# Block-sparse attention and a two-matrix expert layer on one Trainium2 core: four weight blocks ahead instead of five, copies of v and of whole rows laid out anew, two splits issued sooner

## The chip, the cores and the metric

The kernel runs on one core of a Trainium2 chip. The time is that of the device for one execution, in microseconds (us). A core has a matrix engine (PE, with its weight loads shown as PEld), a vector engine (DVE), a scalar engine (ACT), a general engine (POOL), a queue engine for transfers (SP) and 16 DMA engines. Each engine takes its own instructions in the order in which they were written; semaphores tie the engines to each other. Operands of PE, DVE, ACT and POOL lie in an on-chip memory (SBUF) of 128 partitions, and PE writes its sums into another one (PSUM), here eight banks of 128 x 512 fp32.

## What is computed

```python
scores = scale * q @ k.T            # 4 batches, 8 heads, 768 tokens, head size 64
mask   = |block_i - block_j| <= 1  or first/last block row or column  or sampled block
attn   = softmax(where(mask, scores, -1e9))     # blocks of 32 tokens, 24 block rows,
x      = (attn @ v) as 3072 x 512               # three sampled blocks per block row
out    = (max(x @ w_in, 0) ** 2) @ w_out        # w_in 512 x 2048, w_out 2048 x 512
```

The sampled blocks are data. The weights come in double precision and are cut to fp32 on the chip.

## The kernel before

The 3072 tokens are 24 tiles of 128 (six to a batch), and three tiles make a chunk; there are eight chunks c = 0..7. Two kinds of work run in one stream on PE.

**The expert layer** of a chunk (`moe`) goes through 16 column blocks f. `hidden(c, f)` is 12 matmuls `ph` of 128x384 (L888): each fp32 operand is split into a high and a low part, and three of the four products are kept. `finish` then makes r (ACT, L909), gh (ACT, L915), gf (DVE, L920) and gl (POOL, L922). `project(c, f)` is 9 matmuls `po` of 128x512 (L941), gh with the high and the low part of w_out's block, gl with the high part; it runs LEAD = 2 blocks behind `hidden`. So at a chunk turn, `project` of blocks 14 and 15 of chunk c-1 stand back to back between `hidden(c-1, 15)` and `hidden(c, 0)`, and nothing but attention can be put between them. Chunk 0 uses plain fp32 for `project` (`po` at L931, on gp from L912), which needs no split of w_out and no gl.

The weights are split by `split` into a tile `wi` or `wo` of two halves: the high part by a CAST (L850 on ACT in chunk 0, L852 on DVE later), the low part by a subtraction on POOL (L853). A split is made anew in every chunk. Where each is issued sets what it stands behind on DVE and POOL. `wi` of block 1 of a chunk is split after the turn has begun (in `moe(c)`, ahead of `project(c-1, 14)`), `wo` of block f just ahead of `hidden(c, f)`.

In the prologue and in chunk 0 the weights are also cut. `cut_next` runs a little pipeline over 32 raw blocks `craw` of 512 KB: the load (L790, on POOL's queue) at step `done`, two ACT operations (`cut`, L806 and L808) AHEAD steps later, two bit operations on DVE (`cut_bits`, L817 and L818) one step after that. Raw blocks, splits `wi` and `wo`, and the rows `pg`, `pgm` of whole blocks share WBUFS = 7 buffers of one tag, `w`, which go round in the order of request.

**Attention.** The rows of a tile are done in two halves (`Half`; q block rows 1..22 with their eight key blocks), the rows of a batch's first and last block, which see all keys, in four `Whole` units. A half goes through scores `s` (PE, L436), row maxima `m` and `p` = s - m (DVE, L448 and L457) or the exponent on ACT (L498), exponents and block copies `pm` (ACT, L482), a transpose (DVE, L488; in the prologue and for the halves of tiles 3 to 5 on PE with copies `pT`, L523 on ACT and L525 on DVE), values `pv` (PE, L534) and a norm (DVE, L548 to L551). A whole unit goes through `g` (PE, L629), maxima (DVE, L643 to L647), exponents `pg` (ACT), `move` (16 copies `pgm` of 32x192, L665, eight on POOL and eight on ACT), a transpose `pTg` (DVE, L671), `pvg` (PE, L699) and a norm (L710 to L718).

**What sets the order.** The program is written in its final order by hand: `moe(c)` is a generator that yields some 96 times a chunk, and at each yield the `Stream` of attention takes one step. A unit starts at the step that `units` gives it: a half every 16 steps, beginning EARLY = 23 steps ahead of the chunk before; whole unit i of an even chunk G_AT steps after half i. LAG says how many steps lie between a unit's parts ("t" from `g` of a whole unit to its `move`, "w0" and "w" to its transpose and its values). Attention of chunk c thus runs under the expert layer of chunk c-1. Attention of chunk 0 is a prologue, with units every five steps; in it the V tiles are filled by POOL, by ACT (`fixed`, L212) and by sampled DMAs on SP (L365), whose offsets are read from a table.

PSUM's tag "s" of five banks is shared by `ph`, `s`, `g`, `pv` and `pvg`, in turn; three banks hold `po`.

Of the kernel before, what the change touches and what calls it, by code (L numbers as in the profile page):

```python
# [52 lines left out]
AHEAD = 5  # L53
# [12 lines left out]
LAG = {"s": 0, "e": 4, "v": 11, "x": 4, "t": 4, "c": 0, "v0": 13, "w0": 4, "w": 19, "n": -1}  # L66

G_AT = 6
# [7 lines left out]
CUT_0 = range(30, 61, 5)  # L76
CUT_1 = 3
# [4 lines left out]
FIXED_0 = 14  # L82
# [14 lines left out]
def tile_block_sparse_attention_moe(ctx: ExitStack, tc, kd, knd, qd, qgd, vd, vnd, samp, const, wcat, out):  # L97
# [282 lines left out]
    class Half:  # L380
# [63 lines left out]
        def maxima(self):  # L444
# [7 lines left out]
            if not self.moved:  # L452
                if self.k >= UC:
                    nc.vector.tensor_scalar(m[at], m[at], -SCALE, None, op0=ALU.mult)
                return
# [36 lines left out]
        def exps(self):  # L492
            at = self.rows
            if self.k < UC:
                nc.scalar.mul(self.m[at], self.m[at], -SCALE)
            for e in range(2):
                for i in range(2):
                    nc.scalar.activation(  # L498
                        self.p[at, 2 * e + i].rearrange("p c a s -> p (c a s)"),
                        self.sb[e][at, i * NSLOT : (i + 1) * NSLOT],  # L500
                        AF.Exp,
                        scale=SCALE,
                        bias=self.m[at, e, i : i + 1],
                    )
# [81 lines left out]
    class Whole:  # L586
# [71 lines left out]
        def move(self):  # L658
# [3 lines left out]
            for g in range(NJ):  # L662
                for a in range(NJ):
                    copy = nc.scalar.copy if a % 2 else nc.gpsimd.tensor_copy
                    copy(self.pm[a * BLK : (a + 1) * BLK, g], x[g * BLK : (g + 1) * BLK, :, a])  # L665
                    if a % 2:
                        yield 0
# [59 lines left out]
    def units(c):  # L727
# [9 lines left out]
        both += [(at + i * STEP + G_AT, u) for i, u in enumerate(wholes)]  # L737
# [226 lines left out]
    def moe(c):  # L964


        if 0 < c < NCH:
            for i in range(UC):
                high(c, i, 0, NCC, nc.scalar.copy)
                low(c, i, 0, NCC)  # L970
        if c > 0:
            yield 0.7
            if c < NCH:
                wi1[c, 1] = split(c, W1[1], f"wi{c}_1")
# [7 lines left out]
        for f in range(NF):  # L982
            for n in (f, f + 1) if f == 0 else (f + 1,):
                if n < NF:
                    if c == 0:
                        need(n, 0)
                    if n in SINGLE and (c, n) not in wi1:
                        wi1[c, n] = split(c, W1[n], f"wi{c}_{n}")
            if c == 0 and f == 0:
# [6 lines left out]
            if c > 0:  # L996
# [35 lines left out]
    def prepare():  # L1032
# [7 lines left out]
        load_sampled(2, 1, nc.sync, SP, (0, 1))  # L1040
        key_windows(2, 1, nc.gpsimd.tensor_copy)
        deque(keys[2], 0)
        for f in windows(2, 1):
            f(nc.gpsimd.tensor_copy)
# [8 lines left out]
    while work.todo or work.running:  # L1053
        work.step(now)
        now += 1
        if now >= FIXED_0 and fixed:
# [19 lines left out]
    for c in range(NCH + 1):  # L1076
        work.drain(c, now)
        for _ in moe(c):
# [3 lines left out]
            if c == 0 and now % CUT_1 == 0 and done < len(cuts) + AHEAD + 2:  # L1082
# [64 lines left out]
```

## Time and profile before

| | us |
|---|---|
| three timed runs | 742.28, 743.63, 744.39 (median 743.63) |
| the profiled execution's own time | 742.05 |
| its span, first to last instruction | 740.2 |
| PE busy | 706.8 (95%) |
| PEld, weight loads beside PE | 566.4 (77%) |
| POOL busy | 550.6 (74%) |
| DVE busy | 528.7 (71%) |
| ACT busy | 503.9 (68%) |

The mean granted clock of PE is 0.998 of full speed. The prologue, attention of chunk 0, lasts to about 53 us of the span; chunk 0 of the expert layer to about 156; the turns into chunks 2 to 7 lie at about 245, 328, 417, 500, 589 and 672; after 640 there is no attention left. In a list of instructions, the figure in brackets is how long the engine stood idle before the row, with what ended it. PE's matmuls are pipelined, so that one row's duration overlaps the next one's start.

### The profile page before, as it was taken

What the parts mean: (1) busy time and instruction counts of PE and PEld (TensorE: products, weight loads), DVE (VectorE), ACT (ScalarE), POOL (GpSimd) and SP (SyncE); (2) the same over time, 40 slices, a digit from 0 to 9 for tenths busy, and PEclk for the clock granted to TensorE, in tenths of its full rate; (3) what the DMA queues carried; (4) which work ended last, traced back from release to release, by engine and by line L of the source; (5) the groups of instructions that cost most, each with busy time, mean ns of one, the idle gap of its engine ahead of it and who ended that gap; (6) DMA issues with size and microseconds to landing.
All of it is one profiled execution on the core that took longest, in us unless ns stands there. A gap on an engine that the chain in (4) does not pass through costs nothing.

```text
span 740.2 us, 21520 instructions
## 1 busy us (share of the span) xinstructions
PE 706.8 (95%) x7496; PEld 566.4 (77%) x7496; DVE 528.7 (71%) x1062; ACT 503.9 (68%) x1116; POOL 550.6 (74%) x710
## 2 busy tenths in 40 slices
PE   5769999999999999999999999999999999999997
PEld 2546665668788888877878888887778888889895
DVE  5787767868686868668776877768777686647542
ACT  6976777988865866589776776578776767532222
POOL 8978839348876677869777577777877577868984
PEclk9999999999999999999999999999999999999999
DMA  9786798555635565646445467555455352101001
GB/s 282 211 255 172 227 323 245 143 143 158 179 97 134 164 176 159 150 105 158 130 127 136 103 190 196 156 115 158 104 157 145 93 163 49 33 1 43 1 1 43
DMA packets 92784, 104.05 MB, mean 141 GB/s; under 512 B 13667, under 2 KB 80484, under 8 KB 92676
## 3 DMA queue, kind: packets, MB, share of 16 engines
q1 hardware_dynamic: 86724, 79.82, 40.9%
q0 software_dynamic: 5664, 22.45, 9.2%
q8 instruction: 60, 0.98, 0.6%
q14 instruction: 48, 0.39, 0.2%
q10 hardware_dynamic: 288, 0.39, 0.1%
HBM read 96.32 MB, written 6.29 MB: 139 GB/s over the span
## 4 chain that ended last, share of the span: by engine, by line
PE 71%; DVE 9%; ACT 8%; DMA 4%; POOL 3%; SPq 3%; issue 2%; ACTq 0%; POOLq 0%; DVEq 0%
PE ph L888 30%; PE po L941 27%; PE pv L534 5%; PE s L436 5%; DMA V<-in_v_dram 3%; PE po L931 2%; DMA q<-in_q_dram 2%; SPq L365 2%; ACT craw L808 1%; DVE m L448 1%; PE pvg L699 1%; PE g L629 1%; ACT p L498 1%; ACT r L909 1%; POOL gl L922 1%
## 5 line engine op out<-in xcount | busy, mean ns | idle before, releaser
L888 PE MATMUL ph<-xh,wi 128*128 128x384 f32 x960 | 275.1, 347 | 0.2 <-ACT p L498 0.2
L482 ACT ACTIVATE pm<-p 32x256 f32<-32x256 f32 x528 | 219.2, 415 | 15.1 <-DVE p L457 7.9
L941 PE MATMUL po<-wo,gh 128*128 128x512 f32 x672 | 211.7, 396 | 0.1
L853 POOL TENSOR_TENSOR wi<-W,wi 128x512 fp32r<-128x512 f32 x120 | 163.4, 1362 | 62.8 <-DVE wi L852 37.9
L888 PEld LDWEIGHTS ph<-xh,wi 128*128 128x128 f32 x960 | 174.1, 188 | 22.4 <-issue 12.0
L909 ACT ACTIVATE r<-ph 128x384 f32<-128x384 f32 x128 | 63.0, 492 | 167.5 <-PE ph L888 167.0
L853 POOL TENSOR_TENSOR wo<-WO,wo 128x512 fp32r<-128x512 f32 x112 | 144.7, 1292 | 34.4 <-DVE wo L852 33.1
L922 POOL TENSOR_TENSOR gl<-gf,gh 128x384 fp32r<-128x384 f32 x112 | 118.8, 1061 | 64.6 <-DVE gf L920 55.8
L888 PE MATMUL ph<-xl,wi 128*128 128x384 f32 x480 | 161.8, 337 | 0.0
L941 PEld LDWEIGHTS po<-wo,gh 128*128 128x128 f32 x672 | 123.0, 188 | 27.1 <-issue 7.5
L941 PE MATMUL po<-wo,gl 128*128 128x512 f32 x336 | 134.5, 400 | 5.0 <-POOL gl L922 4.9
L920 DVE SCALAR_TENSOR_TENSOR gf<-ph,r 128x384 f32<-128x384 f32 x112 | 62.0, 554 | 108.0 <-ACT r L909 100.0
L888 PEld LDWEIGHTS ph<-xl,wi 128*128 128x128 f32 x480 | 90.2, 188 | 8.9 <-issue 5.2
L852 DVE CAST wo<-WO 128x512 fp32r<-128x512 f32 x112 | 86.3, 771 | 0.0
L941 PEld LDWEIGHTS po<-wo,gl 128*128 128x128 f32 x336 | 63.0, 187 | 24.7 <-POOL gl L922 11.4
L915 ACT ACTIVATE gh<-r 128x384 fp32r<-128x384 f32 x112 | 58.9, 526 | 10.1
L534 PEld LDWEIGHTS pv<-V,pT 128*32 128x32 f32 x2816 | 43.2, 110 | 29.0 <-ACT pT L523 12.6
L448 DVE TENSOR_REDUCE m<-s 128x2 f32<-128x512 f32 (+1 forms) x96 | 61.0, 675 | 2.7 <-PE s L436 2.7
L534 PE MATMUL pv<-V,pT 128*32 128x65 f32 x2816 | 52.6, 223 | 9.5 <-ACT pT L523 6.5
L852 DVE CAST wi<-W 128x512 fp32r<-128x512 f32 x105 | 60.2, 574 | 0.0
L436 PE MATMUL s<-KG,q 64*32 64x256 f32 x1408 | 53.4, 382 | 1.0 <-ACT pT L523 1.0
L931 PE MATMUL po<-WO,gp 128*128 128x512 f32 x96 | 46.8, 602 | 0.0
(93 smaller groups left out, 770.3 us busy)
## 6 DMA issues: line engine op xcount, KB each, us to landing
craw<-in_w_dram POOLq DMA_DIRECT2D x32, 512.0 KB, 5.2
V<-in_v_dram SPq DMA_DIRECT2D x462, 32.5 KB, 2.3
KG<-in_k_dram SPq DMA_DIRECT2D x189, 64.0 KB, 1.9
V<-in_v_dram SPq DMA_DIRECT2D x28, 390.0 KB, 6.3
KG<-in_k_dram SPq DMA_DIRECT2D x12, 768.0 KB, 5.8
q<-in_q_dram SPq DMA_DIRECT2D x24, 256.0 KB, 2.9
out_dram<-ot SPq DMA_DIRECT2D x22, 256.0 KB, 5.2
V<-in_v_dram SPq DMA_DIRECT2D x16, 292.5 KB, 5.9
```

What stands on the lines that cost most here:

```text
L436: nc.tensor.matmul(self.sb[e][g * BLK : (g + 1) * BLK, i * NSLOT : (i + 1) * NSLOT], q[r, j, pr, :], kg[r, j, :, pr, :], start=True, stop= ...
L448: nc.vector.tensor_reduce(m[at, e], self.sb[e][at].rearrange("p (i c) -> p i c", i=2), axis=AX, op=ALU.max)
L482: nc.scalar.activation(p[a * BLK : (a + 1) * BLK, g], x[g * BLK : (g + 1) * BLK, :, a], AF.Exp, scale=SCALE)
L534: nc.tensor.matmul(po[h * BLK : (h + 1) * BLK, g * VW : (g + 1) * VW], self.pT[:, g, 2 * e + i, c], v[:, self.u, j, h * VW : (h + 1) * VW] ...
L852: nc.vector.tensor_copy(w[:, 0], src)
L853: nc.gpsimd.tensor_tensor(w[:, 1], src, w[:, 0], op=ALU.subtract)
L888: nc.tensor.matmul(ph[c, f][:, :TOK], wi[:, w, cc], x[:, cc], start=(cc == 0 and i == 0), stop=(cc == NCC - 1 and i == 2),)
L909: nc.scalar.activation(r, acc[:, :TOK], AF.Relu)
L920: nc.vector.scalar_tensor_tensor(gf, acc[:, :TOK], 0.0, r, op0=ALU.max, op1=ALU.mult)
L922: nc.gpsimd.tensor_tensor(gl, gf, gh, op=ALU.subtract)
L931: nc.tensor.matmul(acc[c][u], g[:, u * P : (u + 1) * P], WO[f], start=(f == 0), stop=(f == NF - 1))
L941: nc.tensor.matmul(acc[c][u], g[:, at], w[:, k], start=(f == 0 and i == 0), stop=(f == NF - 1 and i == 2))
```

## The change

1. AHEAD is 4, not 5. Each raw block is cut one step of the pipeline sooner after its load; `prepare` issues four loads first, not five; CUT_0 has four steps in the prologue, not seven, and CUT_1 steps every second yield for the first 12 yields of chunk 0 and every third after that.
2. FIXED_0 spreads ACT's nine copies into V and the loads after them over the steps 10 to 31 of the prologue (before: one at every step from 14 on). In `prepare` POOL's window copies of the last V tile go ahead of the last key copies.
3. The scaling of `m` by -SCALE for the halves of tiles 3 to 5, six instructions, goes from DVE (L454) to ACT (L495).
4. `move` yields after each of 12 copies, not after each of 8. LAG "t", "w0" and "w" are shortened so that "t" + `move` + "w0" + "w" stays 35. G_AT is a table: whole units start 6, 30, 50 and 68 steps after the first half rather than 6, 22, 38 and 54.
5. At a chunk turn, `wo` of block 0 is split before xh and xl of the new chunk are made, and `wi` of block 1 of the next chunk is split at f = 15 of the chunk before, ahead of `project(c, 13)`, rather than after the turn.

The instructions of PE are the same in number and kind; they stand in another order. DVE has six fewer, ACT six more.

```diff
--- before.py
+++ after.py
@@ -50,7 +50,7 @@
 TOK = UC * P
 LEAD = 2
 PRE = 4
-AHEAD = 5
+AHEAD = 4
 WBUFS = 7
 
 SINGLE = tuple(range(1, NF))
@@ -63,9 +63,9 @@
 STEP = PIECES // (2 * UC)
 EARLY = 23
 LAST = 4
-LAG = {"s": 0, "e": 4, "v": 11, "x": 4, "t": 4, "c": 0, "v0": 13, "w0": 4, "w": 19, "n": -1}
-
-G_AT = 6
+LAG = {"s": 0, "e": 4, "v": 11, "x": 4, "t": 2, "c": 0, "v0": 13, "w0": 3, "w": 18, "n": -1}
+
+G_AT = (6, 30, 50, 68)
 
 STEP_0 = 5
 STEP_1, FIRST_1 = 12, 4
@@ -73,13 +73,13 @@
 LAG_0 = {"s": 2, "x": 2, "t": 3, "c": 2, "v0": 2, "n": 2, "r": 1, "l": 3, "l0": 8}
 SPLIT_0 = 52
 
-CUT_0 = range(30, 61, 5)
-CUT_1 = 3
+CUT_0 = range(30, 46, 5)
+CUT_1 = {0: 2, 1: 3}
 
 KEYS_0 = 8
 
 
-FIXED_0 = 14
+FIXED_0 = (10, 15, 20, 21, 25, 26, 27, 28, 31)
 KEYS_3 = range(40, 56, 4)
 MOVED = 6
 
@@ -450,8 +450,6 @@
                 )
             self.p = rot.tile([P, 4, 2, NJ, BLK], F32, tag="p", name=f"p{self.name}", bufs=PBUFS)
             if not self.moved:
-                if self.k >= UC:
-                    nc.vector.tensor_scalar(m[at], m[at], -SCALE, None, op0=ALU.mult)
                 return
             for e in range(2):
                 nc.vector.tensor_tensor(
@@ -491,8 +489,7 @@
 
         def exps(self):
             at = self.rows
-            if self.k < UC:
-                nc.scalar.mul(self.m[at], self.m[at], -SCALE)
+            nc.scalar.mul(self.m[at], self.m[at], -SCALE)
             for e in range(2):
                 for i in range(2):
                     nc.scalar.activation(
@@ -663,7 +660,7 @@
                 for a in range(NJ):
                     copy = nc.scalar.copy if a % 2 else nc.gpsimd.tensor_copy
                     copy(self.pm[a * BLK : (a + 1) * BLK, g], x[g * BLK : (g + 1) * BLK, :, a])
-                    if a % 2:
+                    if a > 0:
                         yield 0
 
         def turn_blocks(self):
@@ -734,7 +731,7 @@
             return [(i * STEP_1 + FIRST_1, u) for i, u in enumerate(halves)]
         at = begins(c - 1) - EARLY
         both = [(at + i * STEP, u) for i, u in enumerate(halves)]
-        both += [(at + i * STEP + G_AT, u) for i, u in enumerate(wholes)]
+        both += [(at + G_AT[i], u) for i, u in enumerate(wholes)]
         return sorted(both, key=lambda x: x[0])
 
     class Stream:
@@ -965,13 +962,12 @@
 
 
         if 0 < c < NCH:
+            split_wo(c, 0)
             for i in range(UC):
                 high(c, i, 0, NCC, nc.scalar.copy)
                 low(c, i, 0, NCC)
         if c > 0:
             yield 0.7
-            if c < NCH:
-                wi1[c, 1] = split(c, W1[1], f"wi{c}_1")
             for f in range(NF - LEAD, NF):
                 if c == 1 and f == NF - 1:
                     split_wo(0, f)
@@ -986,6 +982,8 @@
                         need(n, 0)
                     if n in SINGLE and (c, n) not in wi1:
                         wi1[c, n] = split(c, W1[n], f"wi{c}_{n}")
+                elif c + 1 < NCH:
+                    wi1[c + 1, 1] = split(c + 1, W1[1], f"wi{c + 1}_1")
             if c == 0 and f == 0:
                 for n in range(2):
                     yield from half_hidden(c, n, 0, NCC // 2)
@@ -993,7 +991,7 @@
                 split_wo(c, f - 1)
             if f >= LEAD:
                 yield from project(c, f - LEAD)
-            if c > 0:
+            if c > 0 and f > 0:
                 split_wo(c, f)
             yield from hidden(c, f)
 
@@ -1038,10 +1036,12 @@
             f(nc.gpsimd.tensor_copy)
         load_sampled(1, 0, nc.sync, SP, (2,))
         load_sampled(2, 1, nc.sync, SP, (0, 1))
+        for _ in range(NJ):
+            next(keys[2])
+        for f in windows(2, 1):
+            f(nc.gpsimd.tensor_copy)
         key_windows(2, 1, nc.gpsimd.tensor_copy)
         deque(keys[2], 0)
-        for f in windows(2, 1):
-            f(nc.gpsimd.tensor_copy)
 
     fixed = [lambda copy, k=k, i=i: copy_static(k, i, copy) for k in range(UC) for i in range(2)]
     fixed += windows(2, 0)
@@ -1053,7 +1053,7 @@
     while work.todo or work.running:
         work.step(now)
         now += 1
-        if now >= FIXED_0 and fixed:
+        if now in FIXED_0:
             fixed.pop(0)(nc.scalar.copy)
             if not fixed:
                 load_sampled(2, 1, nc.sync, SP, (2,))
@@ -1079,7 +1079,7 @@
             now += 1
             if later and next(later[0], True):
                 later.pop(0)
-            if c == 0 and now % CUT_1 == 0 and done < len(cuts) + AHEAD + 2:
+            if c == 0 and now % CUT_1[now >= 12] == 0 and done < len(cuts) + AHEAD + 2:
                 cut_next()
             if now < begins(c + 1) - LAST:
                 work.step(now)
```

Three places show what moved. The first is on ACT in chunk 0, around the cast of the high part of `wi` of block 4 (an engine's name with a number is the semaphore that an instruction waits for; `W` and `WO` are fp32 blocks after the cut). Before:

```order
L808 ACTIVATE craw_1_1201<-craw_1_1201,below 128x512
L850 CAST wi_4_1522<-W_83 128x512 [waits DVE_49,Activation_49]
L806 ACTIVATE W_1318<-craw_0_1268 128x512 [waits DMASW6_49]
L808 ACTIVATE craw_0_1268<-craw_0_1268,below 128x512
L523 COPY pT_3_0_1547<-pt_3_0_0_1530 128x4x4x32 [waits PE_49]
L909 ACTIVATE r_3_1619<-ph_3_1550 128x384 [waits PE_49]
L912 ACTIVATE gp_3_1621<-r_3_1619 128x384 [waits Activation_49]
```

Now:

```order
L805 ACTIVATE craw_1_1376<-craw_1_1376,below 128x512
L906 ACTIVATE r_2_1513<-ph_2_1485 128x384 [waits PE_49]
L909 ACTIVATE gp_2_1515<-r_2_1513 128x384 [waits Activation_49]
L803 ACTIVATE W_1304<-craw_0_1403 128x512 [waits DMASW6_49]
L805 ACTIVATE craw_0_1403<-craw_0_1403,below 128x512 [waits Pool_49]
L847 CAST wi_4_1526<-W_83 128x512 [waits DVE_49]
L803 ACTIVATE WO_1315<-craw_1_1454 128x512 [waits DMAHW2_49,DMAHW1_49,DMAHW3_49,DMAHW0_49,DMASW7_49]
L805 ACTIVATE craw_1_1454<-craw_1_1454,below 128x512
L520 COPY pT_3_0_1551<-pt_3_0_0_1534 128x4x4x32 [waits PE_49]
```

Before, the cast stands right behind the cut of a w_out block (craw_1), and waits for DVE's bits of a block cut shortly before. Now the Relu and the square of block 2 and a cut of a w_in block stand between the two, one more cut stands between the cast and the copy pT, and the cast waits for DVE's bits of a cut further back.

The second place is on DVE at the turn from chunk 2 to 3, with `m` and `p` of a half, the casts and the gf of blocks 14 and 15. Before:

```order
L920 SCALAR_TENSOR_TENSOR gf_14_5830<-ph_14_5685,r_14_5826 128x384 [waits Activation_49,Pool_49]
L448 TENSOR_REDUCE m_0_1_5836<-s_0_1_0_5768 96x2 [waits PE_49]
L448 TENSOR_REDUCE m_0_1_5836<-s_0_1_1_5769 96x2 [waits PE_49]
L457 TENSOR_TENSOR p_0_1_5839<-s_0_1_0_5768,m_0_1_5836 96x512 [waits DVE_49]
L457 TENSOR_TENSOR p_0_1_5839<-s_0_1_1_5769,m_0_1_5836 96x512 [waits DVE_49]
L852 CAST wo_15_5857<-WO_1340 128x512
L488 STREAM_TRANSPOSE pT_0_0_5865<-pm_0_0_5606 128x768
L920 SCALAR_TENSOR_TENSOR gf_15_5892<-ph_15_5860,r_15_5888 128x384 [waits Activation_49,Pool_49]
L876 TENSOR_TENSOR xl_5897<-x_3_4578,xh_5896 128x4x128 [waits PE_49,Activation_49]
```

Now:

```order
L917 SCALAR_TENSOR_TENSOR gf_14_5832<-ph_14_5689,r_14_5828 128x384 [waits Activation_49,Pool_49]
L448 TENSOR_REDUCE m_0_1_5837<-s_0_1_0_5770 96x2 [waits PE_49]
L448 TENSOR_REDUCE m_0_1_5837<-s_0_1_1_5771 96x2 [waits PE_49]
L455 TENSOR_TENSOR p_0_1_5840<-s_0_1_0_5770,m_0_1_5837 96x512 [waits DVE_49]
L455 TENSOR_TENSOR p_0_1_5840<-s_0_1_1_5771,m_0_1_5837 96x512 [waits DVE_49]
L849 CAST wi_1_5843<-W_80 128x512
L849 CAST wo_15_5859<-WO_1326 128x512 [waits PE_49,Pool_49]
L486 STREAM_TRANSPOSE pT_0_0_5867<-pm_0_0_5606 128x768
L917 SCALAR_TENSOR_TENSOR gf_15_5887<-ph_15_5862,r_15_5883 128x384 [waits Activation_49,Pool_49]
L849 CAST wo_0_5891<-WO_86 128x512 [waits PE_49]
L873 TENSOR_TENSOR xl_5895<-x_3_4578,xh_5894 128x4x128 [waits PE_49,Activation_49]
```

The cast of `wi` of block 1 of the coming chunk stands between `p` and the cast of `wo` of block 15; that of `wo` of block 0 between gf of block 15 and the xl.

The third is on POOL at the same turn. Before:

```order
L853 TENSOR_TENSOR wo_14_5682<-WO_1339,wo_14_5682 128x512 [waits DVE_49]
L665 COPY pgm_0_5691<-pg_0_5663 32x192 [waits PE_49,Activation_49,Pool_49]
L665 COPY pgm_0_5691<-pg_0_5663 32x192 [waits Pool_49]
L922 TENSOR_TENSOR gl_14_5832<-gf_14_5830,gh_14_5828 128x384 [waits PE_49,DVE_49,Activation_49,Pool_49]
L665 COPY pgm_0_5691<-pg_0_5663 32x192 [waits Pool_49]
L665 COPY pgm_0_5691<-pg_0_5663 32x192 x3
L853 TENSOR_TENSOR wo_15_5857<-WO_1340,wo_15_5857 128x512 [waits DVE_49,Pool_49]
L665 COPY pgm_0_5691<-pg_0_5663 32x192 [waits Pool_49]
L665 COPY pgm_0_5691<-pg_0_5663 32x192
L922 TENSOR_TENSOR gl_15_5894<-gf_15_5892,gh_15_5890 128x384 [waits PE_49,DVE_49,Activation_49,Pool_49]
L853 TENSOR_TENSOR wi_1_5912<-W_80,wi_1_5912 128x512 [waits DVE_49]
```

Now:

```order
L850 TENSOR_TENSOR wo_14_5686<-WO_1325,wo_14_5686 128x512 [waits DVE_49,Pool_49]
L662 COPY pgm_0_5678<-pg_0_5663 32x192 [waits Pool_49]
L919 TENSOR_TENSOR gl_14_5834<-gf_14_5832,gh_14_5830 128x384 [waits PE_49,DVE_49,Activation_49,Pool_49]
L662 COPY pgm_0_5678<-pg_0_5663 32x192 [waits Pool_49]
L850 TENSOR_TENSOR wi_1_5843<-W_80,wi_1_5843 128x512 [waits DVE_49,Pool_49]
L662 COPY pgm_0_5678<-pg_0_5663 32x192 [waits Pool_49]
L662 COPY pgm_0_5678<-pg_0_5663 32x192
L850 TENSOR_TENSOR wo_15_5859<-WO_1326,wo_15_5859 128x512 [waits DVE_49,Pool_49]
L662 COPY pgm_0_5678<-pg_0_5663 32x192 [waits Pool_49]
L919 TENSOR_TENSOR gl_15_5889<-gf_15_5887,gh_15_5885 128x384 [waits PE_49,DVE_49,Activation_49,Pool_49]
L850 TENSOR_TENSOR wo_0_5891<-WO_86,wo_0_5891 128x512 [waits DVE_49]
```

Between gl of block 14 and gl of block 15 there stands one more split, and two block copies fewer.

## The prediction

> **What bounds the kernel now.** The page comes first, then the table of windows, which says where PE is not busy.
>
> ```profile
> PE 706.8 (95%) x7496; PEld 566.4 (77%) x7496; DVE 528.7 (71%) x1062; ACT 503.9 (68%) x1116; POOL 550.6 (74%) x710
> ```
> ```profile
> 44.00:46.00 2.00, 0.22 (x6) 0.06 (x6) 1.90 (x6) 1.52 (x5) 1.02 (x5) 1.00 0.96 289
> 46.00:48.00 2.00, 1.26 (x48) 1.02 (x48) 1.77 (x3) 2.00 (x4) 1.52 (x5) 0.82 0.94 289
> 48.00:50.00 2.00, 1.55 (x24) 1.14 (x17) 0.68 (x3) 0.01 (x1) 1.26 (x1) 0.50 0.95 280
> 60.00:80.00 20.00, 18.80 (x168) 12.75 (x167) 13.56 (x19) 14.79 (x30) 19.95 (x48) 1.00 0.66 191
> 80.00:100.00 20.00, 18.90 (x193) 12.16 (x190) 15.54 (x25) 15.10 (x29) 13.21 (x27) 1.00 0.82 264
> 100.00:120.00 20.00, 19.66 (x223) 13.71 (x224) 12.30 (x24) 15.06 (x30) 12.11 (x25) 1.00 0.95 292
> 120.00:140.00 20.00, 18.88 (x165) 11.47 (x164) 19.08 (x32) 17.10 (x35) 10.73 (x21) 1.00 0.69 186
> 200.00:220.00 20.00, 18.86 (x218) 15.79 (x217) 14.99 (x34) 13.31 (x32) 16.21 (x15) 1.00 0.38 89
> 360.00:380.00 20.00, 18.86 (x296) 15.21 (x291) 14.54 (x38) 15.57 (x38) 15.76 (x20) 1.00 0.56 155
> 540.00:560.00 20.00, 18.86 (x198) 15.80 (x197) 15.30 (x32) 14.74 (x35) 15.35 (x17) 1.00 0.44 111
> ```
>
> The columns are window, length, then busy time of PE, PEld, DVE, ACT and POOL, the granted clock, the DMA share and GB/s. PE sets the pace of the expert layer, so the 706.8 us cannot shrink (the change keeps every matmul); what can move is the rest. In chunk 0 the four windows leave 1.20 + 1.10 + 0.34 + 1.12 = 3.76 us idle; later, three windows leave 1.14 each; the prologue up to 53 us is a chain of waits. What ended the waits, first from 60 to 140, then from 156 on (total, times, longest):
>
> ```profile
> ACT wi L850 <- DVE WO L818: 9.7, 6, 1.8
> ACT wi L850 <- DVE rec L548: 6.6, 4, 1.8
> PE pv L534 <- ACT pT L523: 2.6, 4, 1.2
> PE s L436 <- ACT pT L523: 1.0, 1, 1.0
> ```
> ```profile
> PE po L941 <- POOL gl L922: 4.9, 8, 1.1
> ```
>
> So chunk 0's loss is PE waiting for ACT's copies pT, 2.6 + 1.0 of the 3.76; the later loss is gl coming late from POOL. ACT itself stands still for 9.7 + 6.6 = 16.3 us ahead of the casts of `wi`, on DVE.
>
> **Chunk 0: AHEAD 4 (gain).** One round on ACT, then PE:
>
> ```profile
> 71.01 0.62 ACT L850 CAST wi<-W 128x512 fp32r<-128x512 f32 x1 [1.72 <-DVE WO L818]
> 71.54 0.67 ACT L806 ACTIVATE W<-craw 128x512 f32<-128x512 f32 x1
> 72.11 0.74 ACT L808 ACTIVATE craw<-craw,below 128x512 int32<-128x512 uint16 x1
> 72.74 0.57 ACT L523 COPY pT<-pt 128x512 f32<-128x512 f32 x1
> ```
> ```profile
> 73.37 1.14 PE L534 MATMUL pv<-V,pT 128*32 128x65 f32 x64 [1.20 <-ACT pT L523]
> ```
>
> The cast waits 1.72 us for DVE's bits of the block that ACT cut directly before it; the cut of the next block (0.67 + 0.74 less overlap, 1.2 us) and pT stand behind, and PE idles 1.20 us for pT. The wait is one for a buffer: six raw blocks under way leave one of seven for a split, and it comes free when those bits are done. With one raw block fewer the cast asks for the bits of a block further back, and other ACT work stands between (the first place shown above). The 1.72 us of waiting exceeds every stall of PE behind it (1.20 at most), so I take all of the 3.76, and 0.1 for each of six stalls, since a matmul after a gap shows 0.50 against 0.40 (rows below): **4.4 us gained**. Bounds: if half the waits stay, 2.2; ACT has to take in three cuts from the prologue and six scalings, so a loss is the second rival, not excluded. The scalings that leave DVE are worth nothing by themselves: they delay bits that, after the change, nobody awaits at once.
>
> **The prologue (near nothing).**
>
> ```profile
> 15.66 2.62 POOL L790 DMA_DIRECT2D craw<-in_w_dram x5
> ```
> ```profile
> 46.27 0.45 PE L534 MATMUL pv<-V,pT 128*32 128x65 f32 x16 [2.04 <-DMA V<-in_v_dram]
> 49.11 1.85 PE L513 MATMUL pt<-ident,p 128*128 128x128 f32 x8
> 65.21 1.06 PE L513 MATMUL pt<-ident,p 128*128 128x128 f32 x8
> ```
> ```profile
> 59.09 0.62 ACT L850 CAST wi<-W 128x512 fp32r<-128x512 f32 x1 [1.21 <-PE ph L888]
> ```
>
> PE waits 2.04 us for the last sampled blocks of V. DMA engines are 96% busy there, at 289 GB/s. One raw block fewer ahead of them (five loads of 512 KB become four) takes 524 KB / 289 GB/s = 1.8 us off the queue; a q load of 256 KB that now stands on SP before the last V loads puts 0.9 back: V lands 0.9 us sooner (0 to 1.8). ACT's later V copies and POOL's earlier window copies hide under this wait of 2.04 us; without it the V copies would delay `pT` by one copy or two, about 1 us. Against that stand the three cuts that moved into the first yields of chunk 0. Of a cut's 1.2 us, three make 3.6; ACT's idle time before 60 us, 1.21 us before the row at 59.09 and two like it, some 3.5 in all, takes in 2.9 by my estimate, so the first `p` and pT of chunk 0 come 0.7 us later. Sum of the prologue: **0.2 gained** (-0.8 to 1.1, and the clock below).
>
> The clock: the window 48 to 50 was granted 0.50, and eight transposes take 1.85 us there and 1.06 at 65.21, so 0.8 us of the chain is half speed. A gap shorter by 0.9 us may keep the clock up; I leave the 0.8 in the range. [...]
>
> **Inside the chunks: `move` and G_AT (gain).**
>
> ```profile
> 200.97 0.91 POOL L665 COPY pgm<-pg 32x192 f32<-32x192 f32 x2
> ```
> ```profile
> 203.00 0.50 PE L941 MATMUL po<-wo,gl 128*128 128x512 f32 x1 [1.14 <-POOL gl L922]
> 335.37 0.50 PE L941 MATMUL po<-wo,gl 128*128 128x512 f32 x1 [0.39 <-POOL gl L922]
> ```
>
> Block copies right ahead of gl make it late: 1.14 us here, and in the same place of chunks 3 and 5. The whole units now start at other steps, with the copies over 12 steps: none of the three places has copies and two splits together. 3 x (1.14 + 0.1) = 3.7 gained; the 0.39 after the turns into chunks 3 and 5, 2 x 0.5 = 1.0. Together **4.7** (2.5 to 4.7: the third and fourth unit's copies have new neighbours, and one of the three could come back).
>
> **The turns: `wi` of block 1 at f = 15 (loss).** Into an even chunk, then an odd one:
>
> ```profile
> 240.34 0.42 DVE L852 CAST wo<-WO 128x512 fp32r<-128x512 f32 x1
> ```
> ```profile
> 240.84 1.30 POOL L853 TENSOR_TENSOR wo<-WO,wo 128x512 fp32r<-128x512 f32 x1 [1.62 <-DVE wo L852]
> 242.71 1.01 POOL L922 TENSOR_TENSOR gl<-gf,gh 128x384 fp32r<-128x384 f32 x1 [0.57 <-DVE gf L920]
> ```
> ```profile
> 243.77 0.50 PE L941 MATMUL po<-wo,gl 128*128 128x512 f32 x1 [0.21 <-POOL gl L922]
> ```
> ```profile
> 321.91 0.59 DVE L852 CAST wo<-WO 128x512 fp32r<-128x512 f32 x1
> ```
> ```profile
> 324.99 1.02 POOL L922 TENSOR_TENSOR gl<-gf,gh 128x384 fp32r<-128x384 f32 x1
> ```
> ```profile
> 326.06 0.50 PE L941 MATMUL po<-wo,gl 128*128 128x512 f32 x1
> ```
>
> PE already waits for gl of block 15 (0.21) or just not (gl ends 326.01, PE starts on it then). The split of `wi` now takes the place of that of `wo` 15 on both engines: behind `p`, its cast ends at 240.8, POOL subtracts to 242.1, then `wo` 15 to 243.4, gl to 244.5, where it was done at 243.72: 0.75 later, at the turns into 2, 4 and 6. Into 3 and 5: cast to 322.4, POOL to 323.7, two copies (0.7), `wo` 15 to 325.7, a copy, gl to 327.1 against 326.01: 1.1 later. Behind it queue `wo` 0 and the next gl, which have time. There too, the scores of the half after the turn take a bank that gf frees, and gf stands on DVE behind the transpose and two copies of the output: 0.5 each, estimated. Sum 3 x 0.75 + 2 x 1.1 + 2 x 0.5 = **5.45 lost** (0 if gl is early enough after all, 8 if the casts wait for POOL too). In exchange the turn itself has one split fewer after it, in POOL's 2 us of idleness: worth nothing. The turns into 1 and 7 have no such neighbours.
>
> **Sum** against the profiled 742.05: 4.4 + 0.2 + 4.7 - 5.45 = 3.85, so 738.2. That execution was 1.6 below the median of the three runs, 743.63, which is what I forecast for: 743.63 - 3.85 = **739.8 us**.
>
> **Rivals.** (1) *The turns are hidden.* If the earlier start of whole units pulls POOL's and DVE's work away from the last blocks of a chunk, the 5.45 shrinks to at most 1 and the clock's 0.8 comes too: 743.63 - 3.85 - 4.45 - 0.8 = 734.5. For it: POOL idles 1.62 us before the row at 240.84. Against: its place behind `p` is fixed by the order. 0.17.
>
> (2) *The raw blocks land too late* (slower). A cut now stands four steps behind its load instead of five.
>
> ```profile
> DMA to landing us min/median/max: 3.7/5.2/12.1
> ```
> ```profile
> 124.74 0.57 POOL L790 DMA_DIRECT2D craw<-in_w_dram  x1
> ```
> ```profile
> 133.81 0.69 ACT L806 ACTIVATE WO<-craw 128x512 f32<-128x512 f32 x1
> 136.84 0.68 ACT L806 ACTIVATE WO<-craw 128x512 f32<-128x512 f32 x1
> ```
>
> These are the raw block's load at 124.74 and its cut at 133.81, 9.1 us later; a step is the 3.0 us between the last two rows, so 6.1 remain, and the median landing is 5.2. From 6.1 on, the cut waits at the head of ACT with r, gp, `p` and pT behind it. Where DMA is 95% busy (100 to 120), a landing of 8 would make it wait 2 us. Four such waits of 2 us, and none of chunk 0's 4.4: 743.63 + 8 - 0.2 + 0.75 = 752; with waits of 1 us, 748. Against: the freed buffer lets loads start sooner, as POOL waited for one. 0.10.
>
> (3) *The waits for the bits merely move.* The cast no longer waits, but pT now stands behind one more cut, and chunk 0 gives 1 rather than 4.4: 743.63 - 0.45 = 743.2, no difference that can be told. For it: two cuts in a row still stand before pT. Against: 16.3 us of waiting are freed for 3.6 of cuts. 0.24, with losses at the turns of 8 counted here.
>
> **How the numbers follow.** The forecast has 0.49, with its own range of 737 to 742.5. About 0.3% of the time, 2.2 us, can be told from no change in a measurement of this kernel: faster is below 741.4, slower above 745.9. Faster: 0.42 of the forecast's 0.49 and rival 1, 0.17, and 0.05 of rival 3: 0.64. Slower: rival 2, 0.10, and 0.02 of rival 3: 0.12. The same: 0.24. The range of 735.5 to 744.8 leaves out half of rival 1 and all of rival 2.
>
> **What would show it.** Right: in chunk 0 the waits of the cast on DVE's bits fall from 16.3 to below 5 us, and PE is busy over 19.7 of 20 in each window from 60 to 140; the windows with 200, 360 and 540 are full; PE waits for gl at each of the five turns, 0.7 to 1.3 us. Wrong: ACT waiting for a DMA ahead of L803 (rival 2); PE still waiting for pT (rival 3); no wait for gl at the turns (rival 1). A prologue that ends much before or after 53 us would show my prologue wrong.

## The result, and the profile after

The changed kernel takes 752.94 us (median of six runs) where the kernel before, on the same chip, took 743.45; the ratio is 1.0121, with a 95% interval from 1.0097 to 1.0145. So it is about 9 us slower, and a gain of 3.85 us was forecast. One of the six runs, of 800.68 us, and one run of the kernel before beside the experiment wi_on_before, of 2384.51 us, fell into a slower state and are left out of the ratios; the other five of the six have a median of 752.85. The profiled execution has a span of 751.1 us against 740.2. PE is busy for somewhat longer, at a lower mean clock (0.987 against 0.998), and DVE for 11.7 us longer though six of its instructions went to ACT:

```profile
PE 714.5 (95%) x7496; PEld 571.0 (76%) x7496; DVE 540.4 (72%) x1056; ACT 503.5 (67%) x1122; POOL 557.7 (74%) x710
```

The table of windows, with the same columns as before:

```profile
46.00:48.00 2.00, 0.86 (x24) 0.62 (x28) 0.23 (x1) 1.82 (x5) 1.12 (x5) 0.51 0.93 278
48.00:50.00 2.00, 0.90 (x32) 0.65 (x24) 0.00 (x0) 0.00 (x0) 1.17 (x1) 0.50 1.08 242
50.00:52.00 2.00, 0.92 (x11) 0.75 (x12) 0.34 (x3) 0.00 (x0) 0.00 (x0) 0.50 0.66 118
54.00:56.00 2.00, 1.91 (x63) 1.74 (x63) 0.09 (x1) 0.04 (x1) 2.00 (x9) 0.50 0.28 65
60.00:80.00 20.00, 18.62 (x181) 11.59 (x166) 16.54 (x21) 17.08 (x33) 17.86 (x38) 1.00 0.62 175
80.00:100.00 20.00, 19.19 (x185) 12.61 (x190) 17.64 (x26) 16.50 (x33) 17.85 (x40) 1.00 0.81 245
100.00:120.00 20.00, 20.00 (x243) 13.67 (x228) 16.58 (x26) 16.18 (x33) 10.49 (x15) 1.00 1.03 352
120.00:140.00 20.00, 20.00 (x177) 12.69 (x176) 19.07 (x25) 16.58 (x33) 14.49 (x31) 1.00 0.79 206
200.00:220.00 20.00, 19.89 (x205) 16.97 (x203) 16.66 (x38) 17.76 (x42) 17.13 (x20) 1.00 0.62 162
240.00:260.00 20.00, 18.36 (x175) 15.18 (x175) 17.57 (x29) 14.70 (x34) 12.19 (x11) 1.00 0.55 160
320.00:340.00 20.00, 17.19 (x164) 12.87 (x153) 16.53 (x32) 12.82 (x30) 13.41 (x16) 1.00 0.56 138
```

Three things stand in it. The end of the prologue is worse: the clock is halved for some ten microseconds, where it was for some three (and for three more from 29 to 32). Chunk 0 is better in its later half (20.00 and 20.00 where 19.66 and 18.88 stood), and the window of 200 to 220, which lost 1.14, is nearly full. And the turns are far worse: the windows 240 to 260 and 320 to 340 lose 1.64 and 2.81, where the kernel before lost 0.21 and 0.44 in them. What ended PE's idle time from 156 on (total, times, longest):

```profile
PE po L938 <- POOL gl L919: 5.2, 5, 1.7
PE ph L885 <- DVE xl L873: 3.2, 4, 0.8
PE po L938 <- POOL wo L850: 2.9, 5, 1.1
```

All fourteen stand at the turns into chunks 2 to 7 (the last of these lies at about 667 us in the kernel before, not at 672). The wait for xl, the low part of the new chunk's input, is one that no step of the prediction had.

### The profile page after: what moved, and what is told of

The parts are those of the page before. It is cut to its first block, busy times and chain, and to the rows that moved or that the text cites. A ratio compares the mean times of both kernels' runs of the same rounds, so it can differ in the third digit from the quotient of the medians.

```text
span 751.1 us, 21529 instructions
## 1 busy us (share of the span) xinstructions
PE 714.5 (95%) x7496; PEld 571.0 (76%) x7496; DVE 540.4 (72%) x1056; ACT 503.5 (67%) x1122; POOL 557.7 (74%) x710
## 5 line engine op out<-in xcount | busy, mean ns | idle before, releaser
L850 POOL TENSOR_TENSOR wi<-W,wi 128x512 fp32r<-128x512 f32 x120 | 166.1, 1384 | 44.7 <-DVE wi L849 22.4
L919 POOL TENSOR_TENSOR gl<-gf,gh 128x384 fp32r<-128x384 f32 x112 | 119.2, 1064 | 93.4 <-DVE gf L917 53.5
L850 POOL TENSOR_TENSOR wo<-WO,wo 128x512 fp32r<-128x512 f32 x112 | 147.8, 1319 | 26.2 <-DVE wo L849 24.3
L849 DVE CAST wo<-WO 128x512 fp32r<-128x512 f32 x112 | 84.5, 754 | 0.0
L531 PEld LDWEIGHTS pv<-V,pT 128*32 128x32 f32 x2816 | 44.9, 113 | 29.2 <-issue 10.9
L531 PE MATMUL pv<-V,pT 128*32 128x65 f32 x2816 | 54.7, 227 | 9.4 <-ACT pT L520 5.7
```

Source lines behind the costliest of these rows:

```text
L531: nc.tensor.matmul(po[h * BLK : (h + 1) * BLK, g * VW : (g + 1) * VW], self.pT[:, g, 2 * e + i, c], v[:, self.u, j, h * VW : (h + 1) * VW] ...
L849: nc.vector.tensor_copy(w[:, 0], src)
L850: nc.gpsimd.tensor_tensor(w[:, 1], src, w[:, 0], op=ALU.subtract)
L919: nc.gpsimd.tensor_tensor(gl, gf, gh, op=ALU.subtract)
```

## The experiments

All times below are medians, and a ratio is to runs of the kernel before on the same chip (742.8 to 743.7 us as a median). Laid one on the other, the parts of the change give a staircase:

| kernel | us | ratio, 95% interval |
|---|---|---|
| AHEAD 4 alone (ahead_alone) | 741.60 | 0.9969 (0.9948 to 0.9990) |
| move and G_AT alone (move_alone) | 739.24 | 0.9953 (0.9936 to 0.9970) |
| both (ahead_move) | 737.14 | 0.9912 (0.9879 to 0.9946) |
| + scalings on ACT (cuts_back) | 737.24 | 0.9910 (0.9883 to 0.9937) |
| + cuts moved into chunk 0 (turns_v_undone) | 738.08 | 0.9944 (0.9928 to 0.9961) |
| + POOL's copies in the new order (fixed_back) | 739.03 | 0.9933 (0.9909 to 0.9957) |
| + ACT's V copies spread (turns_undone) | 740.20 | 0.9958 (0.9942 to 0.9975) |
| + wo of block 0 early (wi_back) | 745.87 | 1.0031 (1.0019 to 1.0044) |
| + wi of block 1 early: the whole change | 752.94 | 1.0121 (1.0097 to 1.0145) |

The rows come from several chips, so a step between two rows is better read from the ratios, times some 743 us, than from the times. By the ratios the turns cost 12.1 us rather than 12.7, and fixed_back lies under turns_v_undone, not above it; the intervals of these two overlap for the most part.

**The turns undone.** Both splits go back to their places, all else stays:

```diff
-            split_wo(c, 0)
...
+            if c < NCH:
+                wi1[c, 1] = split(c, W1[1], f"wi{c}_1")
...
-                elif c + 1 < NCH:
-                    wi1[c + 1, 1] = split(c + 1, W1[1], f"wi{c + 1}_1")
...
-            if c > 0 and f > 0:
+            if c > 0:
                 split_wo(c, f)
```

> The changed kernel with both splits of part 5 back where they were. Theory T (the splits at the turn are the loss): at the turns the trace of the changed kernel shows 2.2 us of stalls into chunks 2, 4, 6, 3.2 and more into 3 and 5 and 0.9 into 7, about 11.4 more than before. They vanish: 752.9 - 11.4, near 741.5 us. Rival R (the block copies in their new steps crowd POOL and DVE at the turn, and the splits only stand among them): the turns stay late, 748 or more.

740.20 us. The two early splits cost 12.1 to 12.7 us, the whole loss and more; rival R falls. Without them the change is faster than the kernel before. The traces say the same of the chunks from 1 on: from PE's first `hidden` matmul of chunk 1 to its last matmul the changed kernel takes 588.9 us and this one 575.9, 13.0 less.

**Only wi back.** The split of `wi` is undone alone:

> The changed kernel with only the split of wi of block 1 back after the turn; wo of block 0 is still split ahead of xh and xl. Theory T: the stalls on wo 15 and gl 15 go (7.6 us), the 0.9 to 1.0 us on xl at four turns stays, since the cast of wo 0 still holds DVE ahead of xl: near 745.3 us. Rival W (the early wo 0 costs nothing by itself, and xl was late only because wi's cast came first): as turns_undone, 741.5.

745.87. So the early `wo` 0 by itself costs 5.7 us, and rival W falls. At the turn into chunk 2 the trace of this kernel has, on DVE and POOL:

```profile
243.82 0.42 DVE L849 CAST wo<-WO 128x512 fp32r<-128x512 f32 x1
244.41 3.56 DVE L873 TENSOR_TENSOR xl<-x,xh 128x512 fp32r<-128x512 f32 x3 [0.17 <-ACT xh L869]
```
```profile
244.08 1.04 POOL L919 TENSOR_TENSOR gl<-gf,gh 128x384 fp32r<-128x384 f32 x1 [0.57 <-DVE gf L917]
245.08 1.74 POOL L850 TENSOR_TENSOR wo<-WO,wo 128x512 fp32r<-128x512 f32 x1
```

and in turns_undone, with the split back, DVE has at the same place:

```profile
244.49 2.43 DVE L873 TENSOR_TENSOR xl<-x,xh 128x512 fp32r<-128x512 f32 x3 [0.50 <-ACT xh L869]
```

The cast itself costs nothing: it fits into DVE's wait of 0.50 us for xh. But the three xl take 3.56 us rather than 2.43 while POOL subtracts for `wo` 0, and POOL's subtraction takes 1.74 rather than 1.29. By the view of one tile, the durations of a single xl (ns, least, median, most) from 156 us on are, in the kernel before and then in this one (whose row takes in two of the turn into chunk 1):

```profile
L876 DVE TENSOR_TENSOR xl<-x,xh x18: 677/680/1243, 243.0 to 666.7; 128x512 fp32r<-128x512 f32 x18
```
```profile
L873 DVE TENSOR_TENSOR xl<-x,xh x20: 676/1248/1782, 155.4 to 671.6; 128x512 fp32r<-128x512 f32 x20
```

At every turn from that into chunk 2 on PE waits 0.8 to 0.9 us for xl.

**The cast early, the subtraction late.** That reading is tested by leaving the cast where it harms nothing and moving only POOL's instruction, to behind `project` of block 15:

```diff
-            split_wo(c, 0)
+            wo0 = rot.tile([P, 2, DM], F32R, tag="w", name=f"wo{c}_0", bufs=WBUFS)
+            nc.vector.tensor_copy(wo0[:, 0], WO[0])
...
+            elif c > 0:
+                nc.gpsimd.tensor_tensor(wo0[:, 1], WO[0], wo0[:, 0], op=ALU.subtract)
+                wo[c, 0] = wo0
```

> As wi_back, but of the early split of wo of block 0 only DVE's cast stays ahead of xl; POOL's subtraction is issued after that of wi of block 1, which waits for a cast behind xl, so POOL stands still while DVE makes xl. Theory L (DVE and POOL hold each other up: xl reads two operands from SBUF while POOL subtracts): xl is back at 2.4 us for three, against 3.6 in wi_back, the 0.8 to 0.9 us stalls on xl at the turns go, near 740.5 us. Rival S (the cast's place in DVE's order is what makes xl late): 745 to 746, xl still late.

739.59, ratio 0.9932 (0.9910 to 0.9955): theory L holds, rival S falls. DVE's cast stands in the same place as in wi_back, and xl has its old length:

```profile
243.71 2.46 DVE L873 TENSOR_TENSOR xl<-x,xh 128x512 fp32r<-128x512 f32 x3 [0.17 <-ACT xh L869]
```

```profile
L873 DVE TENSOR_TENSOR xl<-x,xh x19: 676/680/1256, 155.4 to 664.4; 128x512 fp32r<-128x512 f32 x19
```

No stall on xl is left at any turn.

**Only wo 0 back.** The split of `wo` of block 0 alone goes back behind the turn; that of `wi` stays early.

> The changed kernel with only the split of wo of block 0 back behind the turn; the split of wi of block 1 stays at f = 15. Theory T: the stalls on xl at five turns go, and those on wo 15 and gl 15 stay at 1.3 into even chunks and 2.4 into odd ones, 747 us, so that the two splits add up to the whole. Rival A (the two splits only hurt together): near 742.

751.44, ratio 1.0109 (1.0077 to 1.0140), not 747: with `wo` 0 back, the early `wi` still costs 11.2 us over turns_undone. Rival A falls. Some 1.8 us of the 11.2 lie ahead of chunk 1, which this trace begins at 159.75 us, later than turns_undone (157.97), though the two kernels are the same up to the last block of chunk 0. From chunk 1 on, counted as above, the early `wo` costs 6.0 us (wi_back), the early `wi` 8.8 and both together 13.0. The missing 1.8 are the waits for xl at the turns into 3 and 5, 0.92 and 0.94 in wi_back: where gl is latest, PE no longer waits for xl.

**The early wi on the kernel before.**

```diff
-            if c < NCH:
-                wi1[c, 1] = split(c, W1[1], f"wi{c}_1")
...
+                elif c + 1 < NCH:
+                    wi1[c + 1, 1] = split(c + 1, W1[1], f"wi{c + 1}_1")
```

> The kernel before with only the split of wi of block 1 at f = 15 of the chunk before. Theory C (part of what the changed kernel loses at the turns into 3 and 5 is cover: the scores g of a whole unit, 0.88 us of PE ahead of project 14, went behind the turn, and PE reaches block 15 sooner): the stalls there are 1.0 shorter than the 3.2 us of the changed kernel, those into 2, 4, 6 are the 1.3 as there, about 743 + 3 x 0.9 + 2 x 2.2 = 750 us. Rival D (the split alone makes the whole 3.2): 752 or more. My reckoning ahead of the result (0.75 and 1.1 a turn): 747.5.

752.19, ratio 1.0121 (1.0081 to 1.0160). Rival D holds: this one split, put on the kernel before, makes the stalls into 3 and 5 by itself (0.47 + 2.40 us idle). POOL, DVE and PE at the turn into chunk 3:

```profile
324.56 1.33 POOL L853 TENSOR_TENSOR wi<-W,wi 128x512 fp32r<-128x512 f32 x1 [1.01 <-DVE wi L852]
325.95 1.10 POOL L665 COPY pgm<-pg 32x192 f32<-32x192 f32 x3
327.14 1.29 POOL L853 TENSOR_TENSOR wo<-WO,wo 128x512 fp32r<-128x512 f32 x1
328.49 1.44 POOL L665 COPY pgm<-pg 32x192 f32<-32x192 f32 x2
330.02 1.31 POOL L922 TENSOR_TENSOR gl<-gf,gh 128x384 fp32r<-128x384 f32 x1
```
```profile
324.00 0.41 DVE L852 CAST wi<-W 128x512 fp32r<-128x512 f32 x1
327.40 3.08 DVE L876 TENSOR_TENSOR xl<-x,xh 128x512 fp32r<-128x512 f32 x3 [0.50 <-ACT xh L872]
```
```profile
331.38 0.50 PE L941 MATMUL po<-wo,gl 128*128 128x512 f32 x1 [2.40 <-POOL gl L922]
```

In the kernel before, gl took 1.02 (the prediction's row at 324.99) and the two copies ahead of it 0.72:

```profile
324.14 0.72 POOL L665 COPY pgm<-pg 32x192 f32<-32x192 f32 x2
```

Both had begun before the first xl. The split of `wi` pushes them back, into the time in which DVE makes xl, and there they take 1.44 and 1.31: another 1.0 us. POOL does not stand still from the split of `wi` to the end of gl.

That the stalls come out as long as in the changed kernel (1.13 + 1.66) is partly chance, for the cover of theory C is there. DVE's cast of `wi` begins here 1.55 us ahead of the first matmul of `project` 14 (324.00 and 325.55), and in the changed kernel only 0.54 ahead (324.76 and 325.30), since the 0.88 us of `g` no longer stand between. In return POOL has three copies between the split of `wi` and gl there (1.40 us), and five here (2.54).

**Move and G_AT alone**, on the kernel before:

```diff
-"t": 4, ... "w0": 4, "w": 19
-G_AT = 6
+"t": 2, ... "w0": 3, "w": 18
+G_AT = (6, 30, 50, 68)
...
-                    if a % 2:
+                    if a > 0:
                         yield 0
...
```

> The kernel before with only part 4 (move in 12 steps, the shorter lags, the table G_AT). Theory T: the three waits for gl of 1.14 us inside the chunks go, and the 0.39 after two turns: 743.45 - 4.7, near 739 us. Rival R: the new steps make gl late at the turns, 746 or more.

739.24. PE's waits for gl after 150 us fall from 4.9 us in eight to this (and the second row is new):

```profile
PE po L941 <- POOL gl L922: 1.6, 5, 0.5
PE s L436 <- DVE gf L920: 0.5, 2, 0.3
```

The three long waits inside the chunks are gone. The waits into chunks 3 and 5 did not go but moved: the 0.39 after those turns became 0.48 on gl of block 15 and 0.25 on a bank. Rival R falls.

**AHEAD 4 alone.** The one edit is `AHEAD = 5` to `AHEAD = 4`.

> The kernel before with AHEAD 4 and nothing else. Theory T: the waits of wi's casts on DVE's bits (16.3 us) go and with them the stalls of PE on pT, 4.9 us by their lengths, so 738 to 740 us. Rival P (the casts and pT only wait for something else): 742 or more.

741.60, between the two: the gain is 2.0 us. From 60 to 140 us ACT's waits for DVE's bits fall from 16.3 to 2.8, and new ones for the raw blocks come in, 4.2 us with those of w_out's:

```profile
ACT wi L850 <- DVE W L818: 2.8, 3, 1.3
ACT W L806 <- DMA craw<-in_w_dram: 2.7, 2, 1.4
ACT WO L806 <- DMA craw<-in_w_dram: 1.5, 2, 1.3
```

No stall of PE on ACT's pT is left from 60 to 140 us; in their place PE waits twice for `wi` from POOL (1.2 us), so that its idle time in these windows falls from 3.76 to 1.20 us. At the start of chunk 0, which this trace begins sooner (51.2 us against 52.7), PE waits once for xl, 1.9 us: part of the gain is spent there.

**The prologue.** In turns_v_undone the V copies and POOL's order are as before, on top of turns_undone; in cuts_back the cuts too; in fixed_back only the V copies:

```diff
-FIXED_0 = (10, 15, 20, 21, 25, 26, 27, 28, 31)
+FIXED_0 = 14
...
-        if now in FIXED_0:
+        if now >= FIXED_0 and fixed:
```
```diff
-CUT_0 = range(30, 46, 5)
-CUT_1 = {0: 2, 1: 3}
+CUT_0 = range(30, 61, 5)
+CUT_1 = {0: 3, 1: 3}
```

> The changed kernel with both splits back and also the V copies on ACT and the order of POOL's copies in the prologue as before; the cuts stay. Theory T: the prologue, which ends 3.4 us later in the trace of the changed kernel, gets 2 to 3.4 of it back, so 738 to 739.5 us, and the half-speed stretch of 10 us before 56 us shrinks to one window of 3.4. Rival C (the cuts and the raw loads of AHEAD 4 are what made V land late): no more than 0.5 under turns_undone.

738.08, 2.1 us under turns_undone, on the same chip: the spread V copies and POOL's order cost about that, and rival C falls. The half-speed stretch shrinks from ten microseconds to some seven, not to 3.4 (its length in the trace of the kernel before, 47.3 to 50.7).

> As turns_undone (740.2 us), with the V copies on ACT and the loads after them back at every step from 14 on; POOL's order of copies stays as in the change. Theory F (the loads that follow the last ACT copy, the last V blocks, stand behind a load of q on SP since the copies are spread out, and the ACT copies push pT back): the prologue gets back what turns_v_undone got, 738 us. Rival O (POOL's order did it): 740.

739.03, in the middle, with overlapping intervals on both sides: the times do not tell theory F from rival O. The trace speaks for F. It begins chunk 0 at 54.1 us, like turns_v_undone (53.8), where the five traces with the prologue of the change begin it at 55.5 to 57.3 (wi_back earliest, wo0_back latest). Its SP queue issues the sixteen V loads in one row again, by 43.5 us and ahead of the load of q, where the changed kernel issues the last four from 42.06 to 44.90, behind a load of q at 40.47. It is one trace, and its chunk 0 takes 0.9 us longer than that of turns_undone, for which no cause was found.

> As turns_v_undone, with seven cuts in the prologue and the even pace of three yields in chunk 0 as before; AHEAD 4 stays, so of the change there are AHEAD, the new move with G_AT, and the scalings on ACT. Theory T (the cuts moved into the first yields of chunk 0 made its first p 1.4 us late and took half of what AHEAD 4 gives): the stall before the first pt goes, 738.1 - 1.5, near 736.5 us. Rival (the first p is late from the scaling, or the cuts only return to delay pT in the prologue): 738 or more.

737.24. By the ratios that is 2.5 us under turns_v_undone, by the times 0.8 (on two chips), and 1.5 was expected; the intervals overlap. The stall ahead of the first pt (1.2 us) is gone from its trace, but one of 1.5 us on a `p` near 130 us and one of 0.9 on `wi` stand there: from 60 to 140 us PE idles 2.53 us, where it idled 2.14 in turns_v_undone. So the trace does not show where the gain lies.

> The kernel before with AHEAD 4 and the new move with G_AT, and the scalings on DVE as before: cuts_back (737.2 us) without the scalings on ACT. Theory T (the scalings cost and give nothing): 737.2. Rival M (the scalings on ACT cause the waits for p and for wi in chunk 0 of cuts_back): 735.5. Rival N (the scalings free DVE and that is a good part of the gain): 739 or more.

737.14, as cuts_back: the six scalings are worth nothing that these runs can tell. Rival N falls by the time; rival M by the trace, in which PE still waits for `p` (1.2 us) and for `wi` (1.2) in chunk 0. ahead_move and cuts_back are the fastest kernels of this study, 0.9912 and 0.9910 of the kernel before. They keep AHEAD 4 and the new move, and leave the turns alone.

**The clock.** Into cuts_back go 26 transposes that nothing reads, where PE waits for V, to see whether the granted clock stays up when PE has work there:

```diff
             for g, j in enumerate(self.js):
+                if self.k == UC - 1 and self.u == 0 and g > 0:
+                    for _ in range(16 if g == 1 else 5):
+                        nc.tensor.transpose(po[:, 384:512], ident, ident)
```

> As cuts_back (737.2 us), with 26 transposes into an unused part of the sums' bank where PE waits for the last V blocks in the prologue, 1.75 us ahead of the first wait and 0.55 ahead of two more; nothing reads them. [...]

737.80, no gain. Where the transposes ran, the clock stayed up:

```profile
48.00:50.00 2.00, 2.00 (x38) 1.57 (x40) 0.70 (x2) 1.94 (x4) 0.80 (x4) 1.00 0.98 293
50.00:52.00 2.00, 2.00 (x44) 1.64 (x39) 0.51 (x3) 0.02 (x1) 1.27 (x1) 1.00 1.07 238
54.00:56.00 2.00, 0.64 (x16) 0.29 (x5) 1.97 (x5) 0.35 (x1) 2.00 (x7) 0.96 0.82 197
56.00:58.00 2.00, 2.00 (x6) 2.00 (x7) 1.46 (x5) 0.85 (x2) 2.00 (x9) 0.50 0.63 208
```

At 48 to 52, where cuts_back had 0.50, it is 1.00. But at about 56 us, after the next wait (1.36 us, for xl, with 0.64 us of work in the window), it dropped to 0.50, and V happened to land before PE's fillers were through. This trace is of the slowest of the five runs, 740.38 us, with a mean granted clock of 0.993. In another of them the mean granted clock is 1.000, so that it hardly dropped anywhere; that run took 736.69 us, within the range of cuts_back (735.77 to 738.12). A clock that stays up in the prologue is thus worth nothing that these runs can tell.

## Why the prediction was wrong

**The turns** are the step that failed. The sum had 5.45 us of loss there, with 8 as its bound; undoing them gave 12.1 to 12.7. Two terms were wrong. No rival had such a loss: rival 2 stood at 752 us, close to what was measured, but that is chance, since it put the time into ACT's waits for raw blocks.

*The early `wo` of block 0* was given no price: "Behind it queue `wo` 0 and the next gl, which have time." The working asked who waits for `wo` 0, not what runs beside it. Its subtraction takes POOL's idle time just when DVE makes xl, and xl is what the first matmul of the new chunk waits for. It measured 5.7 us alone. In the changed kernel, at the turn into chunk 2:

```profile
243.51 1.17 DVE L849 CAST wo<-WO 128x512 fp32r<-128x512 f32 x1
244.60 3.79 DVE L873 TENSOR_TENSOR xl<-x,xh 128x512 fp32r<-128x512 f32 x3
```
```profile
244.45 0.50 PE L938 MATMUL po<-wo,gh 128*128 128x512 f32 x1 [0.21 <-POOL wo L850]
245.60 0.50 PE L938 MATMUL po<-wo,gl 128*128 128x512 f32 x1 [0.64 <-POOL gl L919]
248.45 0.44 PE L885 MATMUL ph<-xl,WI 128*128 128x384 f32 x1 [0.79 <-DVE xl L873]
```

*The early `wi` of block 1* had the right mechanism. Counted from the first matmul of `project` 14, the first one with gl of block 15 comes 0.93 us later than before at the turn into 2 (245.60 - 241.77 against 243.77 - 240.87), where 0.75 was worked out. Into 3 and 5 it was put at 1.1 and came out about three times as large: 3.16 into 3 (331.06 - 325.30 against 326.06 - 323.46). In the changed kernel:

```profile
328.91 0.50 PE L938 MATMUL po<-wo,gh 128*128 128x512 f32 x1 [1.13 <-POOL wo L850]
331.06 0.50 PE L938 MATMUL po<-wo,gl 128*128 128x512 f32 x1 [1.66 <-POOL gl L919]
```
```profile
324.76 0.41 DVE L849 CAST wi<-W 128x512 fp32r<-128x512 f32 x1
```
```profile
328.92 0.69 POOL L662 COPY pgm<-pg 32x192 f32<-32x192 f32 x1
329.68 1.32 POOL L919 TENSOR_TENSOR gl<-gf,gh 128x384 fp32r<-128x384 f32 x1
```

Two things make up most of the 2.06 us between. The sum took POOL's durations from rows in which POOL came first; once the chain is later, xl is there before it, and beside xl the last copy takes 0.69 rather than 0.34 and gl 1.32 rather than 1.02: 0.65 us (1.0 in wi_on_before). And part 4 of the change moved the `g` that stood ahead of `project` 14 to behind the turn, so that PE comes to `project` 14 only 0.54 us after the start of the cast behind `p`, which had been 1.55 (321.91 and 323.46): 1.0 us that the sum had put at nothing. The rest is short gaps between POOL's instructions. The 0.5 put on each of these turns for the scores behind it did not come: the changed kernel's trace has no wait of `s` on gf there. The bound of 8 "if the casts wait for POOL too" was on the right track and left out that POOL's own rows are longer beside DVE's xl (gl 1.32 us rather than 1.02).

**The prologue** was put at 0.2 gained and lost 2 to 3 us: chunk 0 begins at 56.0 us in this trace, and at 52.7 before. V did not land 0.9 us sooner. PE's three waits for it, which were 2.04, 0.48 and 0.45 and over at 48.73, were:

```profile
46.28 0.66 PE L531 MATMUL pv<-V,pT 128*32 128x65 f32 x16 [0.30 <-DMA V<-in_v_dram]
47.80 1.09 PE L531 MATMUL pv<-V,pT 128*32 128x65 f32 x32 [0.86 <-DMA V<-in_v_dram]
51.08 0.44 PE L531 MATMUL pv<-V,pT 128*32 128x65 f32 x8 [2.18 <-DMA V<-in_v_dram]
```

over at 51.08, with a DMA share of 0.93 to 1.08 from 46 to 50. One raw block fewer was indeed ahead of V (eight loads issued by 45 us, where there had been nine). But the last V loads, behind the load of q, are issued by 44.90 rather than 44.11, and from there to the end of the wait it took 6.2 us rather than 4.6. So the later issue was seen and the 1.8 us for the raw block were not; why the landing took longer stays open. The half-speed stretch, which the prediction had left in the range as a possible gain of 0.8, became longer (46.1 to 56.3 us, where it was 47.3 to 50.7) and a loss; that a shorter gap alone keeps the clock up, no run shows. With the three cuts moved into chunk 0 PE waits 1.24 us at the first pt, where 0.7 was put; in cuts_back, without them, that wait is gone.

**Chunk 0** was right in its mechanism: ACT's waits for DVE's bits fell from 16.3 to 4.6 + 1.1 = 5.7 us, where "below 5" was the mark, and no stall of PE on ACT's pT is left there. Its size of 4.4 took every stall as a gain. PE's idle time in the four windows fell from 3.76 to 2.19 us (to 1.20 with AHEAD 4 alone), as PE next meets `wi` from POOL (0.41 and 0.39 us) and the late first `p`. Rival 2 was seen, and too small to decide:

```profile
ACT WO L803 <- DMA craw<-in_w_dram: 3.0, 3, 2.0
ACT W L803 <- DMA craw<-in_w_dram: 2.2, 2, 1.3
```

ACT does wait for raw blocks, 5.2 us in five waits, but none of them became a stall of PE: PE's three stalls in these windows, at 69.4, 85.6 and 93.4, all end before the first such wait does, at 97.5.

**Inside the chunks** 4.7 was forecast and move_alone measured 3.6 (742.81 - 739.24): the 3.7 of the three long waits was right, the 1.0 at the turns into 3 and 5 was not, since those waits came back at block 15.

The scalings, worth nothing, were right as far as the runs can tell. The sum, by the staircase's times and by its ratios: 5.8 to 6.5 us gained by AHEAD and the move where 9.1 stood, 3.0 to 3.6 lost by the cuts and the prologue where 0.2 gained stood, 12.1 to 12.7 lost at the turns where 5.45 stood.

## What to carry to other kernels

An idle engine is not free time (here 1.29 us of POOL's idle time cost PE 0.8 to 0.9): before work is moved into POOL's idle stretch, look at what DVE does in the same microseconds, and price both engines' instructions at the length that they have beside each other. When a chain is pushed back, take its durations anew from rows in the company that it will have, not from where it stood. And test a change part by part: two of the parts here were worth 6 us, and two others hid it.

## What the runs showed of the hardware

**DVE and POOL held each other up: three xl took 3.56 us beside POOL's subtraction for `wo` 0 in wi_back and 2.46 without it in wo0_cast_early.** A single xl takes 0.68 us (the median of 18 in the kernel before). The second of the three in wi_back, beside POOL's subtraction for `wo` 0 that begins at 245.08 and ends at 246.82:

```profile
245.58 1.78 DVE L873 TENSOR_TENSOR xl<-x,xh 128x512 fp32r<-128x512 f32 x1
```

It ends at 247.36, 0.54 us after POOL, near the 0.68 of one that had only then begun. POOL's subtraction, 1.29 in turns_undone, had itself stretched to 1.74, and ended 1.2 us after the first xl (244.41 + 1.25). So it looks as if each had waited for the other's instruction to end; that is an estimate from these times, and by what means the two engines hold each other up no run shows. What had not been expected is how little idle time of POOL is worth beside such an operation: 1.29 us of POOL's idle time cost PE 0.8 to 0.9 at each turn. None of it shows as a wait of DVE or POOL; the longer rows are shown as busy time: in the changed kernel six turns with 1.1 to 1.4 us more for xl are the larger part of DVE's added 11.7 us.

**The clock halved where PE was mostly idle, and no one gap tells when.** In the kernel before it was at 0.50 from 47.3 us on, after three waits of 1.26, 0.18 and 2.04 us close together (0.22 us of work in the window 44 to 46); with fillers it stayed at 1.00 from 44 to 54, and halved at about 56, after a gap of 1.36 with 0.64 us of work in the two microseconds around it. But one gap is no measure: in the kernel before a longer one, of 2.34 us, did not halve it, and the granted clock is 1.00 on both sides of it:

```profile
21.23 1.06 PE L699 MATMUL pvg<-vn,pTg 128*64 128x65 f32 x24 [2.34 <-ACT pTg L686]
```

In both traces the drop came after a stretch that was only mostly idle. How much work keeps the clock up, they do not show.
